# Attention matmuls of 128 and 32 columns split over row and column parts of the array

## The chip, the cores and the metric

The kernel runs on one core of a Trainium2 chip. The core's engines are named as in the profile: PE (TensorE, the matmul array; PEld is its loading of weights), DVE (VectorE), ACT (ScalarE), POOL (GpSimd) and SP (SyncE, which here only issues DMAs). The metric is the device time of one execution in microseconds (us).

## What is computed

A linear attention with a decaying state is followed by a feed-forward layer with a cosine gate. There are 4 batches, 8 heads, 768 positions and 48 values a head; the layer goes from 384 to 2048 and back.

```python
for t in range(S):
    cur = einsum('bhd,bhe->bhde', u * k_t, v_t)
    y[:, :, t] = einsum('bhd,bhde->bhe', r_t, state + cur)
    state = w[:, :, None] * state + einsum('bhd,bhe->bhde', k_t, v_t)
x = y, heads side by side, as (B*S, 384)
h = x @ w_in
out = (h * cos(h)) @ w_out
```

## The kernel before

**Chunks.** The positions are cut into chunks of 128, so there are 24 chunks (6 of each batch, chunk i belongs to batch i % 4). Inside a chunk the recurrence is turned into matmuls. k and r are transposed and multiplied by tables of powers of w (L651, L676, L702, L711; late chunks load them in strips and transpose them on DVE, L659, with POOL multiplying, L664). Then, for each of the 8 heads:

- scores: kT by rT, 128 x 128 (`mm_a`, L740). Even and odd heads use the two halves of the rows of the array and write into two PSUM banks, `Ap[0]` and `Ap[1]`. Only entries with key before query count.
- A: ACT writes the identity times r.(u k) of the head into A (`diagonal`, L730), and DVE copies the scores above the diagonal over it (`mask`, L746).
- x: the state times r (`mm_x`, L760) and v times A (`mm_x2`, L773), both with outputs of 32 columns of the array, four column groups in turn, into one bank `xp`. For L760 the state of two heads is first spread by ACT into a buffer `zt` whose other halves are zero (`spread`, L788). ACT casts x to its high part (L796), DVE subtracts for the low part (L801).
- the update of the state: k by v (`mm_z`, L812), then DVE (L820 to L823). The first chunk of a batch has no state yet, and the last needs no update.

**Feed-forward.** Blocks of three chunks (384 columns) go through 16 slices of the hidden layer. A step is nine matmuls for h (L231), a chain of ACT and DVE operations for the gate (L242, L245, L248, L251, L924, L927, L930), and nine matmuls back (L237). All numbers are split into two parts, hence three matmuls for each product.

**Weights.** They arrive as 64-bit words and are converted on ACT, DVE and POOL (L511 to L552); later each piece is loaded again to check its range (L432 to L465).

**Order.** The program does not write its order by hand. `Plan.order` simulates all engines with a cost for each operation and always takes the operation that can start first, the one with the earlier due time among equals. It also gives out the buffers of each ring (`Buf`, `Tile`). Each engine works its list strictly in that order. The first 12 chunks have negative due times and come before the first h; the other 12 are strewn among the steps of the feed-forward part. Early chunks take their PSUM banks from seven (`B_EARLY`), late ones from three (`B_ATT`). While PE has nothing to do before the first h, warm-up matmuls (L989) fill the gap.

**Loads.** SP issues one DMA for each of k, r and v of a chunk (L593, L609). Late chunks load k and r once more in strips, four DMAs each (L614), into the buffers `raw`, of which there are two and which the weights use too.

## Time and profile before

| what | value |
|---|---|
| median of 3 runs | 529.81 us (529.73 to 530.69) |
| the profiled execution's own time | 530.91 us |
| its span, first to last instruction | 529.2 us |
| mean granted PE clock | 0.997 |
| first matmul of the feed-forward part | 64.41 us |

A line of the timeline gives start, length, engine, line and operation, output and inputs, shapes and count; consecutive instructions of one kind are merged. The length of a merged line ends with a modelled end of its last matmul, which overlaps with the next line, so costs are taken from start to start. In the windows, each engine's busy time in the stretch is followed by its number of instructions. In the groups by line, the busy time and the mean time of one come first, then the engine's idle time just before them.

### The profile page before, as it was taken

What the parts mean: (1) busy time and instruction counts of PE and PEld (TensorE: products, weight loads), DVE (VectorE), ACT (ScalarE), POOL (GpSimd) and SP (SyncE); (2) the same over time, 40 slices, a digit from 0 to 9 for tenths busy, and PEclk for the clock granted to TensorE, in tenths of its full rate; (3) what the DMA queues carried; (4) which work ended last, traced back from release to release, by engine and by line L of the source; (5) the groups of instructions that cost most, each with busy time, mean ns of one, the idle gap of its engine ahead of it and who ended that gap; (6) DMA issues with size and microseconds to landing.
All of it is one profiled execution on the core that took longest, in us unless ns stands there. A gap on an engine that the chain in (4) does not pass through costs nothing.

```text
span 529.2 us, 11825 instructions
## 1 busy us (share of the span) xinstructions
PE 515.1 (97%) x4428; PEld 481.2 (91%) x4428; DVE 424.9 (80%) x835; ACT 397.8 (75%) x933; POOL 178.4 (34%) x184
## 2 busy tenths in 40 slices
PE   8999999999999999999999999999989999999995
PEld 6787799999999999999999998999989999999994
DVE  6688788889889787567898999888999889876453
ACT  3888898988789768758687785777857877766664
POOL 6766522265444344233516314033142240400000
PEclk9999999999999999999999999999999999999998
DMA  9887235668756494424675836455445555300001
GB/s 139 143 164 157 66 103 192 197 141 158 148 125 148 117 149 90 76 61 68 125 165 128 170 95 135 105 165 136 112 119 130 167 146 117 96 26 21 1 1 51
DMA packets 114979, 61.60 MB, mean 116 GB/s; under 512 B 78433, under 2 KB 110818, under 8 KB 114914
## 3 DMA queue, kind: packets, MB, share of 16 engines
q1 hardware_dynamic: 109586, 53.50, 41.6%
q0 software_dynamic: 5184, 7.08, 9.4%
q8 instruction: 36, 0.59, 0.5%
q14 instruction: 29, 0.24, 0.2%
q10 hardware_dynamic: 144, 0.20, 0.1%
HBM read 48.96 MB, written 11.80 MB: 115 GB/s over the span
## 4 chain that ended last, share of the span: by engine, by line
PE 81%; DVE 8%; ACT 5%; issue 2%; DMA 2%; POOL 1%; SPq 0%; DVEq 0%; ACTq 0%; POOLq 0%
PE bank L231 33%; PE bank L237 32%; PE bank L740 5%; PE bank L773 5%; PE bank L760 3%; PE bank L651 2%; PE bank L812 2%; DVE gl L930 2%; DMA raw<-in_moe_w_out_dram 1%; DVE f L924 1%; ACT A L730 1%; PE bank L989 1%; ACT gh L927 1%; DVE f L245 1%; ACT f L251 1%
## 5 line engine op out<-in xcount | busy, mean ns | idle before, releaser
L231 PE MATMUL bank<-xh,w_in_hi 128*128 128x384 f32 x384 | 131.8, 343 | 2.8 <-DVE f L924 2.8
L237 PE MATMUL bank<-w_out_hi,gh 128*128 128x384 f32 x384 | 131.4, 342 | 0.5 <-ACT gh L927 0.2
L237 PE MATMUL bank<-w_out_hi,gl 128*128 128x384 f32 x384 | 130.2, 339 | 0.6 <-DVE gl L930 0.6
L237 PE MATMUL bank<-w_out_lo,gh 128*128 128x384 f32 x384 | 129.5, 337 | 0.0
L231 PE MATMUL bank<-xh,w_in_lo 128*128 128x384 f32 x384 | 129.3, 337 | 0.0
L231 PE MATMUL bank<-xl,w_in_hi 128*128 128x384 f32 x384 | 128.8, 336 | 0.0
L924 DVE TENSOR_TENSOR f<-bank,f 128x384 f32<-128x384 f32 (+1 forms) x132 | 71.4, 541 | 36.5 <-ACT f L251 35.9
L930 DVE TENSOR_TENSOR gl<-f,gh 128x384 fp32r<-128x384 f32 (+1 forms) x132 | 84.2, 641 | 14.2 <-ACT gh L927 12.9
L927 ACT CAST gh<-f 128x384 fp32r<-128x384 f32 (+1 forms) x132 | 65.9, 501 | 35.9 <-DVE f L924 33.4
L248 ACT ACTIVATE f<-f 128x384 f32<-128x384 f32 (+1 forms) x132 | 67.6, 514 | 33.2 <-DVE f L245 32.6
L245 DVE SCALAR_TENSOR_TENSOR f<-bank,qi 128x384 f32<-128x384 f32 (+1 forms) x132 | 70.8, 539 | 19.4 <-ACT qi L242 19.0
L242 ACT ACTIVATE qi<-bank 128x384 int32<-128x384 f32 (+1 forms) x132 | 62.3, 475 | 26.7 <-PE bank L231 26.4
L251 ACT ACTIVATE f<-f,quarter 128x384 f32<-128x384 f32 (+1 forms) x132 | 79.6, 605 | 2.1
L231 PEld LDWEIGHTS bank<-xh,w_in_hi 128*128 128x128 f32 x384 | 72.1, 188 | 7.9 <-DVE f L924 4.5
L237 PEld LDWEIGHTS bank<-w_out_hi,gh 128*128 128x128 f32 x384 | 72.0, 187 | 4.5 <-issue 1.6
L237 PEld LDWEIGHTS bank<-w_out_hi,gl 128*128 128x128 f32 x384 | 72.0, 188 | 1.7 <-DVE gl L930 1.5
L231 PEld LDWEIGHTS bank<-xl,w_in_hi 128*128 128x128 f32 x384 | 72.2, 188 | 0.0
L231 PEld LDWEIGHTS bank<-xh,w_in_lo 128*128 128x128 f32 x384 | 72.1, 188 | 0.0
L237 PEld LDWEIGHTS bank<-w_out_lo,gh 128*128 128x128 f32 x384 | 72.0, 187 | 0.0
L730 ACT ACTIVATE A<-ident,a 128x128 f32<-128x128 f32 x192 | 59.3, 389 | 6.3 <-DVE a L721 5.8
L664 POOL TENSOR_TENSOR kT<-kT,decT_k 112x512 f32<-112x512 f32 x12 | 15.6, 1302 | 143.5 <-DVE kT L659 111.8
L542 POOL TENSOR_TENSOR f<-f,raw 128x384 int32<-128x384 int32 x32 | 39.0, 1219 | 65.1 <-DVE f L531 24.8
(88 smaller groups left out, 677.0 us busy)
## 6 DMA issues: line engine op xcount, KB each, us to landing
raw<-in_moe_w_in_dram SPq DMA_DIRECT2D x32, 384.0 KB, 3.3
raw<-in_moe_w_out_dram SPq DMA_DIRECT2D x32, 384.0 KB, 3.2
out_dram<-f POOLq DMA_DIRECT2D x36, 192.0 KB, 5.0
k<-in_k_dram SPq DMA_DIRECT2D x24, 192.0 KB, 3.7
v<-in_v_dram SPq DMA_DIRECT2D x24, 192.0 KB, 4.2
raw<-in_k_dram SPq DMA_DIRECT2D x47, 96.0 KB, 2.3
raw<-in_r_dram SPq DMA_DIRECT2D x47, 96.0 KB, 2.4
out_dram<-f SPq DMA_DIRECT2D x23, 192.0 KB, 3.9
```

Of the source, the lines that this page charges most:

```text
L231: nc.tensor.matmul(ph, a, b_, start=(i == 0), stop=(i == len(mm) - 1))
L237: nc.tensor.matmul(acc, a[:, ts], b_[:, f, :], start=(first and i == 0), stop=(last and i == 2))
L242: nc.scalar.activation(qi, ph, AF.Copy, scale=INV_2PI)
L245: nc.vector.scalar_tensor_tensor(q, ph, INV_2PI, qi, op0=ALU.mult, op1=ALU.subtract)
L248: nc.scalar.activation(q, q, AF.Abs)
L251: nc.scalar.activation(q, q, AF.Sin, scale=-TWO_PI, bias=quarter)
L542: lambda: nc.gpsimd.tensor_tensor(ai(), ai(), cn(), op=ALU.add),
L730: nc.scalar.activation(A[j]()[:, p, :], ident, AF.Copy, scale=ab()[:, h : h + 1])
L740: nc.tensor.matmul(cube(Ap[j])[:, p, :], kT()[ps, p, :], rT()[ps, p, :], start=True, stop=True)
L924: nc.vector.tensor_tensor(g()[:, cs], ph()[:, cs], q()[:, cs], op=ALU.mult)
L927: nc.scalar.copy(gh()[:, cs], g()[:, cs])
L930: nc.vector.tensor_tensor(gl()[:, cs], g()[:, cs], f32(gh())[:, cs], op=ALU.subtract)
```

## The change

The order of the heads in memory changes: the even heads take slots 0 to 3, the odd heads slots 4 to 7. For the odd heads the first and the second 64 positions of a chunk are exchanged when they are loaded, and the transposes use an identity with exchanged halves (`swap`). So while an even head's first half of keys lies in rows 0 to 63, an odd head's second half does.

- **Scores.** Each head becomes two matmuls of 64 keys: the first keys against all 128 queries, the second keys against the last 64 only. The second keys against the first queries, a quarter of the square that never counts, are not computed. Four parts of the array (two halves of rows, two halves of columns) take turns.
- **A** is stored as 64 columns on the diagonal (masked) and 64 columns across (copied by ACT, `across`). `diagonal` writes 64 columns instead of 128.
- **x.** The state is used as it lies in `zc`, so `zt` and `spread` go. State by r and v by A run in eight parts (two halves of rows, four column groups), the two halves of rows into two banks `xp[0]` and `xp[1]`. Two bf16 matmuls with zeros clear the first 64 columns and begin the sums. ACT copies one bank out, DVE adds the other.
- **Order.** In late chunks the update of the state (`mm_z`) follows x in one operation. Loads of k, r and v are three DMAs each, strips eight instead of four, w and u two each. A third raw buffer lies over the early chunks' r buffers, and the ring f has nine buffers.

```diff
-        R_r = ring("r", 2, [P, H, DP], F32)
+        r_all = att.tile([P, 2, H, DP], F32, name="r_all")
+        R_r = [Tile(r_all[:, i]) for i in range(2)]
+        raw_r = Tile(r_all.rearrange("q i h d -> q (i h d)")[:, 0 : 2 * DM].bitcast(I32).rearrange("q (f w) -> q f w", w=2))
...
-        R_f = ring("f", 8, [P, DM], F32)
+        R_f = ring("f", 9, [P, DM], F32)
...
-        R_raw = ring("raw", 2, [P, DM, 2], I32)
+        R_raw = ring("raw", 2, [P, DM, 2], I32) + [raw_r]
-        zc = [att.tile([KP, NP, D], F32, name=f"zc{b}") for b in range(B)]
-        R_zt = ring("zt", 2, [KP, NP, 2 * D], F32)
+        zc = [att.tile([KP, NP, DP], F32, name=f"zc{b}") for b in range(B)]
...
+        def load_w():
+            for a in range(2):
+                src = w.rearrange("(i j a) d -> a i j d", j=2, a=2)
+                nc.sync.dma_start(wr[2 * a : 2 * a + 2, :, 0:D], src[a])
...
+        b_0 = [Buf(B_EARLY) for _ in B_EARLY]
+        def start_banks():
+            for b_ in b_0:
+                nc.tensor.matmul(
+                    b_().rearrange("q (a t) -> q a t", a=4),
+                    warm, warm[:, None, :].to_broadcast([P, 4, P]), start=True, stop=True)
+        op(PE, -300, 1.6, start_banks, [o_dve], b_0)
...
+        def slot(h):
+            return h // 2 + 4 * (h % 2)
+        PARTS = []
+        for g in range(NK * 4):
+            n, m = divmod(g, 3)
+            for h, skip in (((2 * n, 0),), ((2 * n, 32), (2 * n + 1, -16)), ((2 * n + 1, 16),))[m]:
+                PARTS.append((h, skip, g // 4, g % 4))
+        def rounds(n, of, key=lambda x, i: 0):
+            out = {}
+            for g in range(4):
+                for i in range(2):
+                    some = [x for x in PARTS if x[3] == g and of(x, i)]
+                    assert len(some) == n
+                    for t, x in enumerate(sorted(some, key=lambda x: key(x, i))):
+                        out[t, g, i] = (i, *x)
+            return [out[t] for t in sorted(out)]
+        def second(h, i):
+            return i ^ (h % 2)
+        BY_STATE = rounds(2, lambda x, i: slot(x[0]) % 2 == i)
+        BY_V = rounds(4, lambda x, i: True, lambda x, i: second(x[0], i))
+        BY_K = [(0, 0), (2, 1), (1, 0), (3, 1), (2, 0), (0, 1), (3, 0), (1, 1)]
...
+            def load_to(dst, src):
+                t0 = c * C
+                nc.sync.dma_start(dst[:, 0:4], src[b, 0:H:2, t0 : t0 + C, :].rearrange("h t d -> t h d"))
+                for i in range(2):
+                    t1 = t0 + (1 - i) * HC
+                    nc.sync.dma_start(
+                        dst[i * HC : (i + 1) * HC, 4:H], src[b, 1:H:2, t1 : t1 + HC, :].rearrange("h t d -> t h d")
+                    )
...
-                        nc.scalar.activation(A[j]()[:, p, :], ident, AF.Copy, scale=ab()[:, h : h + 1])
+                        nc.scalar.activation(A[j]()[:, p, 0:HC], ident2, AF.Copy, scale=ab()[:, h : h + 1])
...
             def mm_a():
-                for p in range(NP):
+                for p, i in BY_K:
+                    t0 = second(p // 2, i) * HC
                     for j in range(2):
                         ps = slice(j * DP, j * DP + D)
-                        nc.tensor.matmul(cube(Ap[j])[:, p, :], kT()[ps, p, :], rT()[ps, p, :], start=True, stop=True)
+                        nc.tensor.matmul(
+                            cube(Ap[j])[i * HC : (i + 1) * HC, p, 0 : C - t0],
+                            kT()[ps, p, t0 : t0 + HC], rT()[ps, p, t0:C], start=True, stop=True, skip_group_check=True)
...
-                    A[j](), upper[:, None, :].to_broadcast([P, NP, C]), cube(Ap[j])
+                    A[j]()[:, :, 0:HC], upper[:, None, :].to_broadcast([P, NP, HC]), cube(Ap[j])[:, :, 0:HC]
...
+            def across(j):
+                return lambda: nc.scalar.copy(A[j]()[:, :, HC:C], cube(Ap[j])[:, :, HC:C])
...
             def mm_x():
+                for i in range(2):
+                    rows = slice(i * HC, (i + 1) * HC)
+                    nc.tensor.matmul(xv(i)[:, :, 0:HC], warm[rows], warm[rows, None, 0:HC].to_broadcast([HC, NK, HC]),
+                        start=True, stop=False, skip_group_check=True)
+                if c:
+                    state = zc[b].rearrange("q p e -> q (p e)")
+                    for i, h, skip, kk, g in BY_STATE:
+                        p, j = divmod(slot(h), 2)
+                        ps = slice(j * DP, j * DP + D)
+                        at = p * DP + skip
+                        nc.tensor.matmul(xv(i)[G * g : G * g + G, kk, :], state[ps, at : at + G], rT()[ps, p, :],
+                            start=False, stop=False, skip_group_check=True)
+                vf = vb().rearrange("q h d -> q (h d)")
+                for i, h, skip, kk, g in BY_V:
+                    p, j = divmod(slot(h), 2)
+                    rows = slice(i * HC, (i + 1) * HC)
+                    at = slot(h) * DP + skip
+                    t0 = second(h, i) * HC
+                    nc.tensor.matmul(xv(i)[G * g : G * g + G, kk, t0:C], vf[rows, at : at + G],
+                        A[j]()[rows, p, 0 : C - t0], start=False, stop=True, skip_group_check=True)
...
+            def mm_xz():
+                mm_x()
+                if more:
+                    mm_z()
...
+            x_y = op(ACT, due - 0.6, 0.42, lambda: nc.scalar.copy(xs(), xp[1]()[:, 0:DM]), [xo], [xp[1], xs])
+            x_s = op(DVE, due - 0.5, 0.56, lambda: nc.vector.tensor_tensor(xs(), xp[0]()[:, 0:DM], xs(), op=ALU.add),
+                [x_y], [xp[0], xs])
...
```

More of the change, by code (lines that the diff above doesn't have):

```diff
@@ L194 @@
     G = 32
+    HC = C // 2
     NQ = 24
@@ L603, in chunk @@
                 ks, rs = Buf(R_raw), Buf(R_raw)
+            rbs = [rb] if late else [rb, r_first]
             def rn():
@@ new lines, in mm_z @@
+            def mm_z():
+                z = zp()[:, 0 : NP * D].rearrange("q (p e) -> q p e", p=NP)
+                for h in range(H):
+                    p, j = divmod(h, 2)
+                    nc.tensor.matmul(z[j * DP : j * DP + D, p, :], kb()[:, h, 0:D], vb()[:, h, 0:D], start=True, stop=True)
+            more = c < CPB - 1
+            def mm_xz():
+                mm_x()
+                if more:
+                    mm_z()
+            xs = Buf(R_f)
+            x_cost = 0.1 + (0.5 if c else 0.0) + 0.75
@@ new lines, in chunk @@
+            x_after = [e_r, l_v, o_pool, o_dve, *e_A, last_z[b]]
+            if late:
+                zo = xo = op(
+                    PE,
+                    due - 0.7,
+                    x_cost + (0.5 if more else 0.0),
+                    mm_xz,
+                    [o_kd, *x_after],
+                    [rT, *xp, vb, *A] + ([kb, zp] if more else []),
+                    lat=0.3,
+                )
+            else:
+                xo = op(PE, due - 0.7, x_cost, mm_x, x_after, [rT, *xp, vb, *A], lat=0.3)
```

211 lines of the change are left out of this document (118 added, 93 removed).

## The prediction

> **What bounds the kernel now.** I read the page first, then busy time by stretch, then the order of time on PE. The page says which engine to look at, and the chain of work that ended last says the same.
>
> ```profile
> PE 515.1 (97%) x4428; PEld 481.2 (91%) x4428; DVE 424.9 (80%) x835; ACT 397.8 (75%) x933; POOL 178.4 (34%) x184
> PE 81%; DVE 8%; ACT 5%; issue 2%; DMA 2%; POOL 1%; SPq 0%; DVEq 0%; ACTq 0%; POOLq 0%
> ```
>
> PE holds 81% of the chain, so PE time taken out is worth time, if nothing else is close behind. The windows show how close it is (columns: stretch, length, then busy us of PE, PEld, DVE, ACT, POOL).
>
> ```profile
> 16.00:64.00 48.00, 46.82 (x920) 37.49 (x919) 38.33 (x74) 42.18 (x126) 30.96 (x31) 1.00 0.68 132
> 260.00:320.00 60.00, 60.00 (x521) 55.93 (x519) 54.88 (x107) 47.41 (x110) 19.78 (x18) 1.00 0.61 138
> 320.00:380.00 60.00, 59.19 (x511) 55.09 (x502) 53.11 (x100) 43.82 (x101) 17.39 (x15) 1.00 0.50 125
> 380.00:450.00 70.00, 68.33 (x605) 63.48 (x604) 63.27 (x121) 51.32 (x118) 18.06 (x17) 1.00 0.56 138
> ...
> 480.00:529.00 49.00, 42.81 (x242) 41.67 (x240) 24.04 (x57) 29.01 (x70) 0.00 (x0) 0.97 0.04 14
> ```
>
> There are two stages. Up to 64 us the first 12 chunks of the attention run alone: PE is full, ACT at 42.18 of 48 close behind. After it the feed-forward part runs with 12 late chunks strewn in: PE is full, DVE second, at 171.3 of 190 us from 260 to 450. Next, what a chunk costs PE. First the early stage, PE's timeline (start, length, line, count):
>
> ```profile
> 19.15 1.16 PE L740 MATMUL bank<-rT,kT 48*128 48x128 f32 x16
> ...
> 39.43 0.65 PE L651 MATMUL bank<-ident,k 128*112 128x128 f32 x4
> 39.92 0.60 PE L651 MATMUL bank<-ident,r 128*112 128x128 f32 x4
> 40.45 0.86 PE L760 MATMUL bank<-rT,zt 112*32 112x128 f32 x24
> 41.24 1.16 PE L740 MATMUL bank<-rT,kT 48*128 48x128 f32 x16
> 42.33 1.10 PE L773 MATMUL bank<-A,v 128*32 128x128 f32 x32
> 43.37 0.56 PE L812 MATMUL bank<-v,k 128*48 128x48 f32 x16
> 43.86 0.65 PE L651 MATMUL bank<-ident,r 128*112 128x128 f32 x4
> ...
> 61.79 1.16 PE L740 MATMUL bank<-rT,kT 48*128 48x128 f32 x16 [0.36 <-ACT kT L711]
> ```
>
> From start to start a chunk with a state takes 4.43 us of PE (39.43 to 43.86): scores L740 1.09, state by r L760 0.79, A by v L773 1.04, state update L812 0.49, the rest transposes. Chunks 3 to 12 have their scores at 19.15 to 61.79, nine steps of 4.74 us: PE is nearly the pitch there. In the main stage the same bursts stand between matmuls of 384 columns:
>
> ```profile
> 223.39 0.34 PE L237 MATMUL bank<-w_out_lo,gh 128*128 128x384 f32 x1
> 223.66 1.16 PE L740 MATMUL bank<-rT,kT 48*128 48x128 f32 x16
> 224.75 0.44 PE L237 MATMUL bank<-w_out_hi,gh 128*128 128x384 f32 x1
> 225.03 0.34 PE L237 MATMUL bank<-w_out_hi,gl 128*128 128x384 f32 x1
> ...
> 229.34 0.34 PE L237 MATMUL bank<-w_out_lo,gh 128*128 128x384 f32 x1
> 229.61 1.10 PE L773 MATMUL bank<-A,v 128*32 128x128 f32 x32
> 230.64 0.44 PE L231 MATMUL bank<-xh,w_in_hi 128*128 128x384 f32 x1
> 230.92 0.34 PE L231 MATMUL bank<-xl,w_in_hi 128*128 128x384 f32 x1
> ```
>
> A 384-column matmul normally follows the one before by 0.175 us. From 223.39 to 225.03 are 1.64; less two normal steps the scores cost 1.29, which is 0.20 more than their 1.09: that is the price of leaving the full array and coming back. For L773 the same sum is 1.58 - 0.35 = 1.23. With 0.20 added, L760 costs 0.99 and L812 0.69. How many of each fall into the main stage (groups by line, 200 to 480 us):
>
> ```profile
> L740 PE MATMUL bank<-rT,kT 48*128 48x128 f32 x192 | 13.9, 285 | 0.0
> L773 PE MATMUL bank<-A,v 128*32 128x128 f32 x384 | 13.3, 277 | 0.0
> L760 PE MATMUL bank<-rT,zt 112*32 112x128 f32 x288 | 10.4, 277 | 0.0
> L812 PE MATMUL bank<-v,k 128*48 128x48 f32 x128 | 4.5, 212 | 0.0
> ```
>
> 12 bursts each, and 8 of L812: 12 x (1.29 + 0.99 + 1.23) + 8 x 0.69 = 47.6 us.
>
> **The change: PE.** The eight matmuls of the scores leave 16 records, so an f32 matmul is two. L760's 24 records over four column groups are 6 rounds in 0.79, L773's 32 are 8 rounds in 1.04: a round of 128 columns is 0.125, with 0.04 around it. L740's 8 rounds hold only two tiles each and still take (1.09 - 0.04)/8 = 0.131: a round costs what one tile costs, however many tiles are in it. L812's rounds of 48 columns take (0.49 - 0.04)/8 = 0.056; between, 64 columns are 0.070.
> Scores: 16 matmuls in fours, two fours of 128 and two of 64 columns, two records each: 4 x 0.125 + 4 x 0.070 + 0.04 = 0.82; saves 0.27. State by r: 16 matmuls in two rounds of eight, 4 x 0.125 = 0.50. A by v: 32 in four rounds, half of them short, 0.78. The two bf16 matmuls that clear the banks, in another split of the array, aren't in the trace; between 0.04 (the margin of a burst) and 0.40 (two changes of 0.20), I take 0.20, one change. Together 0.20 + 0.50 + 0.78 + 0.04 = 1.52, and now in one burst: 1.72 in the main stage instead of 0.99 + 1.23, saves 0.50. The update follows in the same burst and saves one return, 0.20, eight times. Main stage: 12 x 0.77 + 1.6 = 10.8 us. Early: 12 x 0.27, and for the 8 chunks there with a state (the first chunk of each of the 4 batches has none) 8 x (0.79 + 1.04 - 1.52); without a state 1.02 takes the place of 1.04. That is 3.2 + 2.5 = 5.7.
> A rule against the halves: the Trainium skill, TensorEngine Tiling (Array Packing), Instruction Overhead, says that every matmul carries about 60 cycles and that a dimension already small should not be cut further. If 64 columns cost as much as 128, a chunk would lose 8 x 0.055 = 0.44, some 10 us of the 16 in all. The row of L812 speaks against it: 48 columns take less than half a round of 128.
>
> **The change: ACT and DVE.** The rows by shape:
>
> ```profile
> L730 ACT ACTIVATE A<-ident,a 128x128 f32<-128x128 f32 x192 | 59.3, 389 | 6.3 <-DVE a L721 5.8
> L788 ACT COPY zt<-zc 48x192 f32<-48x192 f32 x40 | 13.9, 348 | 2.1 <-PE bank L760 1.2
> L958 ACT COPY f<-bank 128x384 f32<-128x384 f32 x40 | 18.9, 477 | 4.7 <-PE bank L237 3.8 <-issue 0.5
> L927 ACT CAST gh<-f 128x384 fp32r<-128x384 f32 x126 | 64.3, 511 | 35.8 <-DVE f L924 33.4 <-PE bank L237 1.2 <-PE bank L231 0.7
> L927 ACT CAST gh<-f 128x128 fp32r<-128x128 f32 x6 | 1.6, 292 | 0.1
> L746 DVE COPY_PREDICATED A<-upper,bank 128x512 f32<-128x512 int32 x48 | 34.9, 741 | 8.1 <-ACT A L730 6.4 <-PE bank L812 0.7 <-PE bank L740 0.3
> L924 DVE TENSOR_TENSOR f<-bank,f 128x384 f32<-128x384 f32 x126 | 69.7, 553 | 35.4 <-ACT f L251 34.7
> L924 DVE TENSOR_TENSOR f<-bank,f 128x128 f32<-128x128 f32 x6 | 1.8, 292 | 1.2 <-ACT f L251 1.2
> ```
>
> ACT: 256 columns fewer save 0.22 (L927), so 64 fewer save 0.055, eight times 0.44; the two L788, 0.70, go where there is a state. Two copies of 256 columns come, between 0.292 and 0.477, 0.385 each, and one of 384, 0.477. Net +0.11 with a state, +0.81 without. DVE: two masks of 256 columns, midway between 0.292 and 0.553, 0.42 each instead of 0.741, -0.64; the sum of the two banks +0.55; net -0.09. So neither engine is relieved. The wait for the two new copies is PE's, and behind it stand the feed-forward matmuls; the copies are planned well ahead of it, so I put it at nothing; without that cover it costs up to one copy, 0.4, a chunk.
> The 12 late chunks in 280 us make about 8 between 260 and 450: 8 x 0.9 = 7.2 us less of PE in 190 leaves DVE, with 171.3, at 94%. The range checks among that work can slide behind 450. The way from the last attention matmul to x is one ACT and one DVE operation longer (0.477 + 0.553), at four block starts. For both I take off 1.8 of the 10.8; the bounds are 0, if checks and chain fit into DVE's gaps, and 6.5, if DVE hands back nearly all of the 7.2. 9.0 remain. The buffer that holds the sum of the banks is the ninth of a ring of eight, so it takes none away.
> Early, ACT's 42.18 of 48 grows by about 4 x 0.81 + 8 x 0.11 = 4.1 at most; its cover is the 5.8 us it is idle now. Of PE's 5.7 I take 2.3 (bounds 0 and 5.7), nearer to what ACT leaves, 1.7.
>
> **The change: SP.** A load of r, k or v goes out as three DMAs, a staged load as eight instead of four.
>
> ```profile
> 17.18 0.37 SPq L593 DMA_DIRECT2D k<-in_k_dram  x1
> 17.65 0.52 SPq L609 DMA_DIRECT2D r<-in_r_dram  x1
> ...
> 329.69 1.75 SPq L614 DMA_DIRECT2D raw<-in_k_dram  x4
> ...
> 6.30 0.62 PE L651 MATMUL bank<-ident,r 128*112 128x128 f32 x4 [0.15 <-DMA r<-in_r_dram]
> ```
>
> An issue takes 0.37 to 0.52, and four small ones 1.75: it is paid by the DMA, not by its size. Early: 9 x 0.44 = 4.0 us in a pitch of 4.74, which fits; at 0.52 it is 4.7 and just fits. Late: 25 issues, 11 us, and one chunk every 23 us (12 in 280); a third raw buffer gives them lead. At the very start w goes in two DMAs and five more issues stand ahead of the first r (6.30 in the row, so about 8.5); the decay tables hide most of it, but they start from w. With POOL's longer preparation I take 1.0 of slip (bounds 0 and 2.5).
> **Sum:** -9.0 - 2.3 + 1.0 = -10.3. The profiled execution took 530.91 (span 529.2), so 520.6; it lay 1.1 above the median of the runs, 529.81, and against that the forecast is 519.5.
>
> **The rivals.** *More arrives:* the early stage passes on all 5.7 and DVE costs nothing in the main one: -10.8 - 5.7 + 1.0 = -15.5, 514.3; bursts with less margin reach 512. For it: PE 46.82 of 48. Against: ACT 42.18.
> *The gain stops at DVE and ACT:* main stage 10.8 - 6.5 = 4.3, early stage nothing, slip 1.0: -3.3, 526.5. For it: 54.88 of 60. Against: DVE has 25 idle us after 480, where checks can go.
> *SP becomes the bound of the early stage (slower):* if nine issues of smaller DMAs take 0.65 each they set a pitch of 5.8 instead of 4.74, +11.7 over 11 chunks, and the first loads slip 2.5: -9.0 + 11.7 + 2.5 = +5.2, 535. It decides from about 0.6 an issue. For it: SP works its queue in order and waits there for buffers. Against: 0.37 in most rows.
> *Row and column parts don't run beside each other (slower):* every round of eight or four falls into two. Scores 1.60 (+0.51), the x burst 3.0 against 2.22 (+0.78), main 12 x 1.29 - 1.6 = 13.9, early some 16: +30, 560. It decides from where a new round takes 1.3 old ones. L740 shows two row parts together, L773 four column parts; no row shows both at once. The Trainium skill, TensorE: Matmul & The Clock Gate, Measured speedup vs the span model, gives 10.6 times for 16 parts in both directions, which speaks against this rival.
>
> **How the numbers follow.** Forecast (516 to 523) 0.48; more arrives 0.18; gain stops 0.19; within 0.2% 0.04; SP 0.07; parts not together 0.04. 0.2% is 1.1 us, about what a measurement of this kernel can tell from none. Faster 0.85, same 0.04, slower 0.11. For 8 in 10 the range leaves out the two slower rivals and the edge of the others: 512 to 527.
>
> **What would show it.** Scores' bursts near 0.9 instead of 1.16, one burst of about 1.6 us in place of L760 and L773, with eight starts a round; PE busy 14 to 17 us less. First feed-forward matmul at 62 to 64 instead of 64.41. DVE above 93% from 260 on with few PE gaps. Wrong if rounds of 64 columns take 0.1 or more, if SP issues stand above 0.6, or if PE waits grow by over 6 us.

## The result: slower by 7.4%

| | before | after |
|---|---|---|
| median | 529.81 us | 568.95 us (567.11 to 572.17, 4 runs) |
| ratio, 95% interval | | 1.0741 (1.069 to 1.0792) |
| profiled execution, its span | 530.91, 529.2 | 572.17, 570.4 |
| mean granted PE clock | 0.997 | 0.965 |
| first feed-forward matmul | 64.4 | 94.1 |
| main stage (from it to the start of PE's last instruction) | 458.1 | 468.8 |

So 29.7 us of the 41.2 by which the span grew lie ahead of the first feed-forward matmul, 10.7 in the main stage and 0.8 behind it. First the profile page of the changed kernel, busy time and chain:

```profile
PE 527.1 (92%) x5817; PEld 490.1 (86%) x5817; DVE 444.5 (78%) x861; ACT 398.9 (70%) x967; POOL 183.2 (32%) x188
PE 46%; DVE 17%; SPq 11%; DMA 10%; ACT 8%; issue 4%; POOL 3%; POOLq 0%; DVEq 0%; ACTq 0%
```

PE's share of the chain fell from 81% to 46%. SP's queue and the DMAs, together 2% before, hold 21%. DVE went from 8% to 17%. These are the two places to look at. The windows of the changed kernel say when (stretch, length, busy us of PE, PEld, DVE, ACT, POOL, then PE's clock, DMA share, GB/s):

```profile
16.00:64.00 48.00, 37.21 (x982) 27.82 (x978) 24.91 (x54) 29.43 (x95) 21.05 (x21) 0.87 0.55 98
64.00:94.00 30.00, 25.18 (x653) 20.20 (x654) 16.69 (x35) 16.45 (x54) 14.30 (x14) 0.77 0.49 104
...
290.00:410.00 120.00, 116.11 (x1383) 109.35 (x1363) 113.49 (x213) 87.28 (x207) 39.95 (x35) 1.00 0.59 138
```

In the early stage every engine is idle for long: PE 37.21 of 48, warm-up matmuls included, where it was 46.82, and ACT 29.43 where it was 42.18. And PE's clock is down to 0.87 and 0.77. In the main stage DVE is at 113.49 of 120, and PE has gaps that it didn't have. What the early stage waits for stands in SP's timeline and in the list of waits (engine, line, what it waited for: us, times, longest) of the changed kernel:

```profile
30.73 0.55 SPq L682 DMA_DIRECT2D r_all<-in_r_dram  x1
31.37 1.25 SPq L685 DMA_DIRECT2D r_all<-in_r_dram  x2
32.72 0.56 SPq L682 DMA_DIRECT2D v<-in_v_dram  x1
33.32 1.25 SPq L685 DMA_DIRECT2D v<-in_v_dram  x2
34.69 0.54 SPq L682 DMA_DIRECT2D k<-in_k_dram  x1
35.32 1.25 SPq L685 DMA_DIRECT2D k<-in_k_dram  x2
36.67 1.44 SPq L682 DMA_DIRECT2D r_all<-in_r_dram  x1
```

```profile
POOL f L784 <- DMA r_all<-in_r_dram: 30.7, 9, 5.6
...
PE bank L749 <- DMA r_all<-in_r_dram: 10.5, 12, 2.1
```

SP issues one DMA after the other with hardly a gap. From 30.73 to 36.67 are the three loads of one chunk: 5.94 us for nine issues. PE's timeline at the same time:

```profile
33.04 0.90 PE L839 MATMUL bank<-rT,kT 48*64 48x128 f32 x32
...
37.17 0.71 PE L1133 MATMUL bank<-warm 128*128 128x256 bf16 x5
...
38.98 0.90 PE L839 MATMUL bank<-rT,kT 48*64 48x128 f32 x32
```

From scores to scores 33.04 to 38.98: 5.94 us again. The early stage runs at SP's pace, and PE fills the rest with warm-up matmuls. Over the whole stage the pitch is longer still: the scores of the first and the twelfth chunk start at 11.29 and 90.69, eleven steps of 7.22. SP is at it all the time: the 108 issues of the 12 chunks stand from 2.42 to 84.48, 0.76 each. Ten of them took 0.98 to 1.95, together some 8.5 us more than ten of the others, and PE's clock was at half in several stretches.

PE's own work did become shorter. The bursts of the changed kernel in its main stage:

```profile
262.83 0.34 PE L239 MATMUL bank<-w_out_lo,gh 128*128 128x384 f32 x1
263.10 0.90 PE L839 MATMUL bank<-rT,kT 48*64 48x128 f32 x32
...
264.21 0.34 PE L239 MATMUL bank<-w_out_hi,gl 128*128 128x384 f32 x1
...
269.61 0.34 PE L239 MATMUL bank<-w_out_lo,gh 128*128 128x384 f32 x1
269.88 0.26 PE L870 MATMUL bank<-warm 64*128 64x192 bf16 x2
270.07 0.67 PE L884 MATMUL bank<-rT,zc 48*32 48x128 f32 x32
270.53 1.03 PE L894 MATMUL bank<-A,v 64*32 64x128 f32 x64
271.49 0.56 PE L907 MATMUL bank<-v,k 128*48 128x48 f32 x16
...
272.26 0.33 PE L239 MATMUL bank<-w_out_hi,gl 128*128 128x384 f32 x1
```

Read as in the prediction, the scores cost 264.21 - 262.83 - 0.35 = 1.03 (1.29 before), and the burst of x with the update 272.26 - 269.61 - 0.35 = 2.30 (before 0.99 + 1.23 + 0.69 = 2.91). That is 0.26 for the scores of 12 chunks, 0.61 for the 8 with an update and 0.41 for the 4 without, 9.6 us if every burst were like these. Added up over all bursts of the main stage (below) 6.8 us are saved. More than that is lost elsewhere.

**Three sums used below.** *Gaps*: wherever two feed-forward matmuls follow each other by over 0.15 us more than the normal step of 0.175, the excess, added up over the trace. *Bursts*: for each burst of attention matmuls between feed-forward matmuls the cost as just read, added up; a wait of PE right behind a burst falls in here and not into the gaps. *DVE above normal*: for each DVE instruction after the first feed-forward matmul that took over 0.15 longer than the lower quartile of its line and shape, the excess, added up.

| profiled run | first matmul | main stage | gaps (number) | bursts | DVE above normal |
|---|---|---|---|---|---|
| before | 64.4 | 458.1 | 5.4 (9) | 49.3 | 19.2 |
| after | 94.1 | 468.8 | 17.6 (19) | 42.5 | 36.8 |
| e1, one DMA a load, four strips | 67.9 | 461.6 | 10.8 (14) | 41.7 | 36.9 |
| e12, one DMA a load, eight strips | 68.1 | 464.9 | 16.6 (20) | 41.8 | 36.9 |
| e8, e1 with POOL's addition on DVE | 67.4 | 457.6 | 8.8 (15) | 43.2 | 23.1 |
| e9, e1 with three edits | 68.5 | 463.1 | 8.0 (13) | 48.1 | 23.4 |
| e11, before with joined bursts | 64.3 | 455.3 | 6.9 (13) | 44.5 | 21.6 |

Each row is one execution; those of the changed kernel and of e1 took 3.2 and 2.3 us more than the medians of their runs, so a difference of 2 or 3 us between two rows shows nothing by itself.

### The profile page after: what moved, and what is told of

Its sections match the earlier page's. It is cut to its first block, busy times and chain, and to the rows that moved or that the text cites. A ratio compares the mean times of both kernels' runs of the same rounds, so it can differ in the third digit from the quotient of the medians.

```text
span 570.4 us, 15083 instructions
## 1 busy us (share of the span) xinstructions
PE 527.1 (92%) x5817; PEld 490.1 (86%) x5817; DVE 444.5 (78%) x861; ACT 398.9 (70%) x967; POOL 183.2 (32%) x188
## 4 chain that ended last, share of the span: by engine, by line
PE 46%; DVE 17%; SPq 11%; DMA 10%; ACT 8%; issue 4%; POOL 3%; POOLq 0%; DVEq 0%; ACTq 0%
PE bank L233 20%; PE bank L239 20%; DMA r_all<-in_r_dram 5%; SPq L712 4%; DVE gl L1074 4%; SPq L685 4%; DVE f L1068 2%; SPq L682 2%; DVE f L247 2%; ACT gh L1071 2%; PE bank L894 2%; ACT f L253 1%; ACT f L250 1%; PE bank L839 1%; DVE w_out_lo L605 1%
## 5 line engine op out<-in xcount | busy, mean ns | idle before, releaser
L239 PE MATMUL bank<-w_out_hi,gl 128*128 128x384 f32 x384 | 132.1, 344 | 6.3 <-DVE gl L1074 6.1
L1074 DVE TENSOR_TENSOR gl<-f,gh 128x384 fp32r<-128x384 f32 (+1 forms) x132 | 85.6, 650 | 12.2 <-ACT gh L1071 10.8
L1071 ACT CAST gh<-f 128x384 fp32r<-128x384 f32 (+1 forms) x132 | 65.9, 501 | 41.2 <-DVE f L1068 37.8
L250 ACT ACTIVATE f<-f 128x384 f32<-128x384 f32 (+1 forms) x132 | 67.9, 516 | 34.8 <-DVE f L247 34.1
L247 DVE SCALAR_TENSOR_TENSOR f<-bank,qi 128x384 f32<-128x384 f32 (+1 forms) x132 | 70.7, 538 | 16.9 <-ACT qi L244 16.6
L828 ACT ACTIVATE A<-ident,a 128x64 f32<-128x64 f32 x192 | 50.0, 338 | 5.0 <-DVE a L819 4.9
L1117 POOL DMA_DIRECT2D out_dram<-f x36 | 32.0, 1101 | 42.1 <-ACT f L1102 37.1
```

The costliest lines, as they stand in the source:

```text
L239: nc.tensor.matmul(acc, a[:, ts], b_[:, f, :], start=(first and i == 0), stop=(last and i == 2))
L247: nc.vector.scalar_tensor_tensor(q, ph, INV_2PI, qi, op0=ALU.mult, op1=ALU.subtract)
L250: nc.scalar.activation(q, q, AF.Abs)
L828: nc.scalar.activation(A[j]()[:, p, 0:HC], ident2, AF.Copy, scale=ab()[:, h : h + 1])
L1071: nc.scalar.copy(gh()[:, cs], g()[:, cs])
L1074: nc.vector.tensor_tensor(gl()[:, cs], g()[:, cs], f32(gh())[:, cs], op=ALU.subtract)
```

## The experiments

The theory after the result: in the early stage SP's issues are the pace, and in the main stage PE waits for DVE, which is held up by DMAs and by POOL. The rivals: the exchange itself is dear (transposes with `swap`, copies), the plan's wrong numbers spoil the order, or the small DMAs are slow on the way rather than at SP. All ratios are against runs of the kernel before on the same chip.

### e1_one_dma: one DMA a load, four strips

```diff
-                nc.sync.dma_start(dst[:, 0:4], src[b, 0:H:2, t0 : t0 + C, :].rearrange("h t d -> t h d"))
-                for i in range(2):
...
+                nc.sync.dma_start(dst, src[b, :, c * C : (c + 1) * C, :].rearrange("h t d -> t h d"))
```

> The changed kernel, but r, k and v are loaded by one DMA each and the strips by four, as before; heads and halves then lie in the natural order, so the values are those of other heads and positions. Theory SP (the number of DMAs that SP issues, about 0.65 us each in a row, holds the early stage, and its lateness puts the planned order out of step later): first feed-forward matmul at 60 to 65 us instead of 94, time 515 to 525. Rival PE (the smaller matmuls themselves or the longer way to x cost the time): still above 550, first feed-forward matmul above 85.

Measured: 537.95 us (535.82 to 540.25), ratio 1.0155 (1.0121 to 1.0189). The first feed-forward matmul came at 67.9, so 26.2 of the 29.7 us belong to the split of the loads. But neither the time nor the first matmul reached the ranges expected (515 to 525, 60 to 65): the main stage, 461.6, is still longer than before, though its bursts are as short as in the changed kernel. Its longest gap, in the timeline of e1:

```profile
126.23 3.22 DVE L605 TENSOR_TENSOR w_out_lo<-f,w_out_hi 128x384 fp32r<-128x384 f32 x1
126.40 2.62 POOL L595 TENSOR_TENSOR f<-f,raw 128x384 int32<-128x384 int32 x2
129.38 0.54 DVE L1061 TENSOR_TENSOR f<-bank,f 128x384 f32<-128x384 f32 x1
...
129.97 0.69 PE L233 MATMUL bank<-xh,w_in_hi 128*128 128x384 f32 x1 [2.81 <-DVE f L1061]
```

A DVE subtraction that normally takes 0.55 took 3.22: as long as POOL's two additions beside it. Behind it in DVE's queue stood the gate's multiplication L1061, behind that PE, 2.81 us. None of these lines belongs to the change. In the kernel before no gap between feed-forward matmuls is longer than 1.83 us; that it is the new order alone that makes them meet is argued, not shown (e7). The Trainium skill, SBUF — State Buffer, section SBUF: two separate sides, describes such a wait: DVE and GpSimd share a pair of SBUF ports under an exclusive lock for a whole instruction, and a DVE operation with two SBUF operands takes part in it when the GpSimd operation reads SBUF. The row agrees so far: both operands of L605 are in SBUF, while L1061, which reads a bank, keeps its 0.54. That L605 is held through two of POOL's operations, though it started before the first, is not said there; the row shows it.

Behind the gap PE is slow for a while (windows of e1):

```profile
129.00:136.00 7.00, 6.03 (x19) 6.03 (x20) 6.17 (x13) 4.85 (x11) 0.02 (x1) 0.52 0.53 141
136.00:143.00 7.00, 7.00 (x42) 7.00 (x40) 5.03 (x11) 5.65 (x14) 4.00 (x5) 0.99 0.59 101
```

From 129 to 136 PE's clock is 0.52. Of these 7 us the first 0.97 are the end of the gap; in the rest there are 19 matmuls at 0.32 each, which would take 3.3 us at the normal step. That the gap brought this about is not shown: another gap of the same length had no such stretch behind it (last section).

### e2_before_split: the kernel before with three DMAs a load

```diff
+                nc.sync.dma_start(dst[:, 0:4], src[b, 0:4, t0 : t0 + C, :].rearrange("h t d -> t h d"))
+                for i in range(2):
+                    t1 = t0 + i * 64
+                    nc.sync.dma_start(dst[i * 64 : (i + 1) * 64, 4:H], src[b, 4:H, t1 : t1 + 64, :].rearrange("h t d -> t h d"))
```

> The kernel before with nothing changed but that each load of r, k and v is three DMAs of the same bytes. Theory SP: the pitch of an early chunk goes from 4.7 to 6.5 us, first feed-forward matmul at 85 to 95, time 550 to 565. Rival PE: SP has room, as the prediction said; within 5 us of 529.8.

Measured: 555.69 us (552.91 to 558.04), ratio 1.0509 (1.0455 to 1.0563), first feed-forward matmul at 89.2, main stage 457.6. Nothing but the split of the loads differs from the kernel before, and 25 us of the early stage's loss are there. Its SP queue:

```profile
30.68 0.55 SPq L594 DMA_DIRECT2D v<-in_v_dram  x1
31.33 1.25 SPq L597 DMA_DIRECT2D v<-in_v_dram  x2
32.69 0.55 SPq L594 DMA_DIRECT2D k<-in_k_dram  x1
```

One load from start to start (30.68 to 32.69) is 2.0 us, as in the changed kernel. So the exchange has no part in it. Nor are the small DMAs slow on the way (issues by tile, KB each, median us from issue to landing; the kernel before, then e2):

```profile
k<-in_k_dram SPq DMA_DIRECT2D x24, 192.0 KB, 3.7
```

```profile
k<-in_k_dram SPq DMA_DIRECT2D x48, 48.0 KB, 2.5
```

Once issued they land sooner than the large ones; it is the issuing that takes the time.

### e3_no_exchange: the changed kernel with the heads in natural order

```diff
-            return h // 2 + 4 * (h % 2)
+            return h
...
-            return i ^ (h % 2)
+            return i
...
-                    nc.tensor.transpose(d[0:KP, p, :], flat(src, p), ident if p < 2 else swap)
+                    nc.tensor.transpose(d[0:KP, p, :], flat(src, p), ident)
```

Loads, strips, w and u go as before; `zc` gets 16 columns in front.

> The changed kernel without the exchanged halves: heads in natural order, the halves of rows carry unequal numbers of columns, all loads as before (one DMA, strips four, one for w and u). Theory SP: about as fast as with one DMA and exchange, 517 to 527, scores about 1.0 us instead of 0.85, v by A hardly slower because the issue of 64 records, 0.015 us each, holds it already. Rival PE: above 550.

Measured: 541.18 us (540.23 to 541.68), ratio 1.0224 (1.0194 to 1.0253); first matmul at 71.2, main stage 462.4, gaps 10.6. A miss. Without the exchange two long rounds no longer meet, so the scores take 1.02 from start to start; but the 14 us by which it misses the range can't come from that. Exchange and loads are both taken back here and the main stage stays long, so they aren't all of its loss. The early stage too is late with the loads of before: PE's clock was at half for 6.8 us from 11.3 on, behind a pause. The clearing of the banks ahead of it was the suspect, and e6 tests it.

### e4_plan_told: the changed kernel, the plan told what SP's issues cost

```diff
-                l_ks = op(SP, due - 6.2, 2.2, load_s(ks, k), ahead, [ks], lat=4.0, line=ln)
+                l_ks = op(SP, due - 6.2, 3.9, load_s(ks, k), ahead, [ks], lat=4.0, line=ln)
...
-            l_k = op(SP, due - 5.2, 1.35, load(kb, k), ahead, [kb], lat=2.6, line=ln)
+            l_k = op(SP, due - 5.2, 2.1, load(kb, k), ahead, [kb], lat=2.6, line=ln)
```

> The changed kernel with nothing changed but the costs that the planner takes for SP: 2.1 instead of 1.35 us for a load, 3.9 instead of 2.2 for strips. Theory SP with the plan out of step: the early stage stays at 90 to 95 us, the main stage, 469 us now, loses 5 to 15, time 553 to 565. Rival (the main stage is lost to the loads themselves or to the longer way to x): no change, 565 to 573.

Measured: 568.3 us (566.83 to 569.89), ratio 1.0742 (1.0703 to 1.0781). Against the 568.95 of the changed kernel that is nothing, as the rival had it (565 to 573). A miss for the theory that knowing the price helps: work that SP can't do in time isn't made less by another order. (The other three costs, of r's strips and of loading r and v, changed in the same way.)

### e5_sum_in_bank: x from the bank

```diff
-                lambda: nc.vector.tensor_tensor(xs(), xp[0]()[:, 0:DM], xs(), op=ALU.add),
+                lambda: nc.vector.tensor_tensor(xp[0]()[:, 0:DM], xp[0]()[:, 0:DM], xs(), op=ALU.add),
```

> The kernel of e1_one_dma (each load one DMA, so its numbers aren't the reference's), with one thing changed: DVE writes the sum of the two banks back into the bank instead of into SBUF, and the high and the low part of x are taken from the bank, so the subtraction for the low part no longer reads two operands from SBUF. Theory A, the longer way to x costs the main stage through the port that DVE and POOL share: DVE's time above normal after the first feed-forward matmul falls from 36.9 us to 30 or less, the main stage from 461.6 to 457 to 460, total 533 to 536. Theory B, the collisions come from the order in which the plan puts everybody's work, the new operations add little to them: 33 to 40 us above normal, main stage 459 to 465, total 536 to 541.

Measured: 535.06 us (533.81 to 540.78), ratio 1.0098 (1.0071 to 1.0125). The subtraction for the low part, in the changed kernel and in e5 (groups by line: busy, mean ns):

```profile
L950 DVE TENSOR_TENSOR xl<-f,xh 128x384 fp32r<-128x384 f32 x24 | 17.1, 714 | 2.0 <-ACT xh L945 2.0
```

```profile
L943 DVE TENSOR_TENSOR xl<-bank,xh 128x384 fp32r<-128x384 f32 x24 | 13.2, 550 | 0.4 <-ACT xh L938 0.3
```

With one operand from the bank it takes 550 ns, as before the change (24 in 13.2 us), with two from SBUF 714 on average. DVE above normal fell to 25.8 and the main stage to 458.6, both as theory A said, and so is the total. The profiled run took 540.78, 5.7 above the median, with two stretches of half clock in the early stage, so its first matmul, 70.9, isn't typical of the median.

### e6_start_later: banks cleared behind the transposition of w

```diff
-        op(PE, -300, 1.6, start_banks, [o_dve], b_0)
...
+        for b_ in b_0:
+            op(PE, -94, 0.23, start_bank(b_), [o_dve, o_wT], [b_])
```

> The kernel of e1_one_dma with the seven matmuls that clear the banks at the start moved behind the transposition of w (one operation a bank instead of one for all). Theory A, they hold up the decay tables by about 1.2 us, and the pause before the first scores costs as much again: first feed-forward matmul at 65 to 66.5 instead of 67.9, total 1.5 to 3 us less than 537.95 if the main stage stays. Theory B, the first stage is late for another reason (more instructions on PE, the longer way to x): first feed-forward matmul still 67 to 68.5.

Measured: 536.08 us (535.44 to 537.75), ratio 1.0127 (1.0099 to 1.0155), first matmul at 66.8: between the two theories. Of the 3.5 us by which e1 starts its main stage late, 1.1 go with the clearing, by one profile each. Where the other 2.4 lie is open. The main stage changed as well, 458.3, though nothing of it was touched but the order that the plan makes of it.

### e7_before_told: the kernel before, one planned cost changed

```diff
-            last_A[0] = o_A = op(PE, due - 1.7, 1.1, mm_a, [e_k, e_r], [kT, rT, *Ap], lat=0.3)
+            last_A[0] = o_A = op(PE, due - 1.7, 0.8, mm_a, [e_k, e_r], [kT, rT, *Ap], lat=0.3)
```

> The kernel before with the same work, one number of the plan changed: the scores of a chunk are planned at 0.8 us instead of 1.1, as the changed kernel plans them. Theory order: the kernel before owes part of its time to an order that happens to keep DVE and POOL apart; with another order DVE's time above normal in the main stage rises from 19.2 us to 25 to 38, PE's stalls from 5.4 to 8 to 12, total 532 to 538. Theory work: the order matters little and the time stays at 529 to 531.

Measured: 532.09 us (530.33 to 533.2), ratio 1.0049 (1.0028 to 1.0069). The time is in the range of the theory of order, but not for its reason: DVE above normal stayed at 17.8 and the gaps at 5.3. The new order put the first feed-forward matmul at 52.5, with chunks left over for the main stage, which grew to 471.0. So the order alone moves this kernel by half a per cent, and a difference of 2 or 3 us between two runs of this study may be no more than that. That the changed order alone brings the collisions of DVE and POOL isn't shown by it.

### e8_add_on_dve: POOL's addition moved to DVE

```diff
-                POOL,
...
-                lambda: nc.gpsimd.tensor_tensor(ai(), ai(), cn(), op=ALU.add),
+                DVE,
...
+                lambda: nc.vector.tensor_tensor(ai(), ai(), cn(), op=ALU.add),
```

> The kernel of e1_one_dma with the 32 additions of the weights' conversion moved from POOL to DVE (DVE's sum of integers can lose their lowest bits, so the numbers aren't the reference's). Up to about 260 us POOL then has little besides the attention, and the long waits of DVE behind it at 113.4, 126.2 and 164.5 can't come. Theory A, the stalls of PE up to 260 us are DVE waiting for POOL: DVE's time above normal between 64 and 260 falls from 15.3 to 6 or less, stalls from 10.8 to 4 to 7, the stretch of half clock at 129.3 goes, main stage 453 to 457, total 530 to 534. Theory B, DVE itself is what PE waits for: 17.6 us more work on DVE make the stalls longer, main stage 462 to 470, total 538 to 546.

Measured: 534.12 us (533.0 to 538.86), ratio 1.0104 (1.0066 to 1.0143). DVE above normal between 64 and 260 us fell from 15.3 to 0.9, the gap at 126 and the half clock behind it are gone, and the main stage fell by 4.0 to 457.6, though DVE got 32 additions more. So the waits behind POOL were a real cost, and DVE's own work wasn't the bound there. Total and main stage end just above theory A's ranges. The gaps are 8.8 and not the 4 to 7 expected: those behind 260 us, where POOL works for the attention, stayed (22.2 us of DVE above normal).

### e9_together: the three edits at once

```diff
+                lambda: nc.vector.tensor_tensor(xp[0]()[:, 0:DM], xp[0]()[:, 0:DM], xs(), op=ALU.add),
...
+            op(PE, -94, 0.23, start_bank(b_), [o_dve, o_wT], [b_])
...
+                lambda: nc.vector.tensor_tensor(ai(), ai(), cn(), op=ALU.add),
```

> The three edits of e5_sum_in_bank, e6_start_later and e8_add_on_dve together, on the kernel of e1_one_dma (the numbers aren't the reference's, for the reasons given there). Theory A, the longer way to x, the clearing at the start and DVE's waits behind POOL are three separate losses: they add up, 537.95 less 2.9, 1.9 and 3.8 gives 529.4, so 528 to 532, with a main stage of 453 to 456. Theory B, each edit only gave the plan another order, and the gains don't add: 533 to 537.

Measured: 540.95 us (538.05 to 542.47), ratio 1.0213 (1.018 to 1.0245). Above the ranges of both theories: the gains don't add, and the three edits together are no faster than none. The first feed-forward matmul came at 68.5, the main stage took 463.1. DVE above normal did fall, to 23.4, and the gaps to 8.0. One of them alone is 2.9 us long (timeline of e9):

```profile
448.97 1.61 POOL L755 TENSOR_TENSOR rT<-rT,decT_r 112x512 f32<-112x512 f32 x1
449.35 2.63 DVE L509 TENSOR_TENSOR f<-f,f 128x384 f32<-128x384 f32 x1
450.53 1.03 POOL L785 TENSOR_TENSOR k<-k,dec_k 128x384 f32<-128x384 f32 x1
...
454.22 0.44 PE L233 MATMUL bank<-xh,w_in_hi 128*128 128x384 f32 x1 [2.74 <-DVE f L1060]
```

It is the same pattern with other lines: L509, an operation of the range check, sits through two of POOL's, and the gate waits behind it. Two longer waits stand right behind bursts, so they are in the 48.1 of the bursts (e1: 41.7):

```profile
75.27 0.45 PE L233 MATMUL bank<-xh,w_in_hi 128*128 128x384 f32 x1 [3.37 <-ACT w_in_hi L600]
...
297.78 0.44 PE L233 MATMUL bank<-xh,w_in_hi 128*128 128x384 f32 x1 [3.17 <-DVE f L1060]
```

The second is the gate again. The first is another kind, a piece of the weights that ACT hasn't converted yet. So the plan's new order brought waits of its own, not all of them of DVE behind POOL.

### e10_before_two: the kernel before with two DMAs a load

```diff
+                nc.sync.dma_start(dst[:, 0:4], src[b, 0:4, t0 : t0 + C, :].rearrange("h t d -> t h d"))
+                nc.sync.dma_start(dst[:, 4:H], src[b, 4:H, t0 : t0 + C, :].rearrange("h t d -> t h d"))
```

> The kernel before with each load of r, k and v in two DMAs (four heads each). Theory A, an issue of SP in an unbroken row costs 0.6 to 0.65 us whatever its size: six of them take 3.6 to 3.9 us of a pitch of 4.74, they fit, first feed-forward matmul at 64 to 67, total 529 to 532.5. Theory B, splitting itself is what hurts (later arrival, smaller transfers): half of the 26 us of e2_before_split, first feed-forward matmul at 72 to 78, total 537 to 543.

Measured: 527.75 us (526.74 to 528.58), ratio 0.9968 (0.9951 to 0.9984), first matmul at 64.5. That is below theory A's range and far from theory B's. Six issues a chunk fit, nine of e2's kind don't: the loss sets in between, as a bound does, and splitting by heads costs nothing. The Trainium skill, DMA: Bandwidth & Descriptors, section Rules for kernel authors, advises one transfer over 128 partitions in place of two to halves of them. The loads of the change do the opposite for the odd heads, and e2, which does so too, lost 25 us; e10, split by heads over all partitions, lost nothing. But e2 has nine issues and e10 six, so no run tells the halves from the number. Its SP queue has gaps:

```profile
34.93 0.37 SPq L594 DMA_DIRECT2D v<-in_v_dram  x1
35.39 0.46 SPq L595 DMA_DIRECT2D v<-in_v_dram  x1
36.52 0.75 SPq L594 DMA_DIRECT2D k<-in_k_dram  x1
```

The second of two loads here mostly takes 0.46 to 0.50 right behind the first, the halves of e2 and of the change 0.59 to 0.62. An estimate from these rows: nine issues of e10's kind, 0.55 from start to start, would be 4.95 us, a little more than the pitch of 4.74, and not 5.94.

### e11_before_joined: the joined bursts alone

```diff
+            def mm_xz():
+                mm_x()
+                mm_x2()
+                if more:
+                    mm_z()
...
+                zo = xo2 = op(PE, due - 0.7, 1.83 + (0.5 if more else 0.0), mm_xz, ...)
```

(State by r only where there is one; for late chunks alone.)

> The kernel before with one part of the change alone: in the late chunks the state by r, v by A and the update of the state are one operation of PE, so they stand in one burst; loads, scores and x are as before. Theory A, a border between the attention and the feed-forward matmuls costs 0.19 us: 44 bursts become about 25, which saves 3.6 us of the main stage, 458.1 to 453.5 to 455.5, total 525 to 527.5. Theory B, the new order costs as much in waits of PE as the borders save: main stage 457 to 462, total 528.5 to 533.

Measured: 526.99 us (526.03 to 529.72), ratio 0.9965 (0.9947 to 0.9983). The time is that of theory A, and the main stage, 455.3, is at the upper end of its range. The timeline:

```profile
228.04 0.34 PE L237 MATMUL bank<-w_out_lo,gh 128*128 128x384 f32 x1
228.31 0.86 PE L760 MATMUL bank<-rT,zt 112*32 112x128 f32 x24
228.99 1.08 PE L773 MATMUL bank<-A,v 128*32 128x128 f32 x32
230.00 0.56 PE L799 MATMUL bank<-v,k 128*48 128x48 f32 x16
...
230.78 0.34 PE L237 MATMUL bank<-w_out_hi,gl 128*128 128x384 f32 x1
```

230.78 - 228.04 - 0.35 = 2.39. The eight parts, two banks, two more copies and the sum of the change reach 2.30 for the same work. So of the 0.61 by which this burst became shorter, 0.52 came from joining and 0.09 from the parts.

### e12_strips_eight: which DMAs the main stage minds

```diff
-                nc.sync.dma_start(dst[:, 0:4], src[b, 0:H:2, t0 : t0 + C, :].rearrange("h t d -> t h d"))
...
+                nc.sync.dma_start(dst, src[b, :, c * C : (c + 1) * C, :].rearrange("h t d -> t h d"))
```

The loads' edit of e1_one_dma alone; the eight strips stay.

> The changed kernel with each load of r, k and v as one DMA in natural order, and its eight strips kept (heads of loads and strips don't match, so the numbers aren't the reference's); e1_one_dma has four strips as well. It tells where the 7.2 us lie by which the changed kernel's main stage (468.8) is longer than that of e1_one_dma (461.6). Theory strips, DVE's transposition waits for eight DMAs that SP issues too slowly, and the gate's operations stand behind it: the main stage stays at 465 to 469, a transposition waits over 1 us for its strips, total 541 to 546. Theory loads, it is the 25 issues of a late chunk together, and 19 are few enough: no such wait, main stage 460 to 463, first feed-forward matmul at 67 to 69 in both cases, total 536 to 540.

Measured: 542.41 us (541.7 to 543.02), ratio 1.023 (1.0201 to 1.0259). Strips: 4.5 us more than e1 by the medians (4.0 by the ratios), and two transpositions wait for them, 2.79 and 1.4 us. Ahead of the first the last strip landed 4.5 us after its issue at 179.82, and the transposition started at 184.64. The same in the changed kernel itself:

```profile
203.26 3.70 SPq L712 DMA_DIRECT2D raw<-in_r_dram  x8
...
211.30 1.08 DVE L757 STREAM_TRANSPOSE rT<-raw 128x512 f32<-128x512 f32 x1 [2.50 <-issue]
...
212.23 0.53 DVE L1074 TENSOR_TENSOR gl<-f,gh 128x384 fp32r<-128x384 f32 x1
```

```profile
212.82 0.66 PE L239 MATMUL bank<-w_out_hi,gl 128*128 128x384 f32 x1 [2.24 <-DVE gl L1074]
```

The eight strips of r leave SP until 206.96, the transposition that needs them starts at 211.30, and DVE does nothing for 2.50 us ahead of it. The gate's subtraction stands behind it in DVE's queue, and PE waits 2.24 us. The main stage of e12, 464.9, ends just under the range of that theory (465 to 469). The other 3.9 us up to the changed kernel's 468.8 are 1.0 of gaps, 0.7 of bursts and for the rest half clock: 10.2 us of the changed kernel's main stage had it and 3.4 of e12's. Why isn't known.

### e13_joined_two: e10 and e11 together

```diff
+                nc.sync.dma_start(dst[:, 4:H], src[b, 4:H, t0 : t0 + C, :].rearrange("h t d -> t h d"))
...
+                zo = xo2 = op(PE, due - 0.7, 1.83 + (0.5 if more else 0.0), mm_xz, ...)
```

> The kernel before with the two edits that made it faster together: one burst for x and the update in late chunks (e11_before_joined, 526.99 against 529.41) and two DMAs a load (e10_before_two, 527.75). If the two gains are separate they add: 2.4 and 1.7 give 525.3, so 524 to 526.5, first feed-forward matmul at 64 to 65, main stage 453.5 to 455.5. If the gain of the two DMAs was only another alignment of DVE and POOL, it doesn't add: 526.5 to 529.

Measured: 526.8 us (525.15 to 531.12) beside 530.01 of the kernel before on that chip, ratio 0.9947 (0.9924 to 0.9969); main stage 454.1. If the gains added, the ratio would be 0.9965 x 0.9968 = 0.9933, and that lies in the interval; but so does that of one edit alone, 0.9965. The time lies in the range for gains that don't add (526.5 to 529), the main stage in the other. Whether they add stays open. e10, e11 and e13 are the versions that beat both kernels, by 0.3 to 0.5%.

## Why the prediction was wrong

- **The step that failed is SP's term**, "Early: 9 x 0.44 = 4.0 us in a pitch of 4.74, which fits". The rows of 0.37 and 0.52 were issues with pauses around them, and the four strips, 0.44 each, were DMAs of another form: in a row of eight they take 0.46 each in the changed kernel too (203.26, 3.70). The loads of the change take 0.54 to 0.62 in their unbroken row, and 0.05 to 0.1 passes to the next issue, which the sum left out: nine took 5.94. The rival *SP becomes the bound of the early stage* named the mechanism and, with 0.65 an issue, the price; the measured pitch of 5.94 is its 5.8. It was given 7%, with the argument "0.37 in most rows" against it (18 of the 36 loads), and those rows don't show the state that the change makes. Nor was 0.6 an issue needed: 4.74 over nine is 0.53 from start to start. Its +14.2 was also too small: the stage got 29.7 longer. Eleven steps longer by 1.2 are 13.2 of that, the ten longer issues some 8.5; the rest, half clock among it, wasn't told apart.
- **The early saving of PE, 2.3, did not arrive either.** With one DMA a load (e1) the first feed-forward matmul came 3.5 later and not 1.3 earlier. From 16 to 64 us PE spends 6.5 on warm-up matmuls there, before 3.8, so at least part of the time that PE saved went into filling. What holds the stage instead is open.
- **Scores, state, x: right.** 1.03 where 0.82 + 0.20 was forecast, 2.30 for x with the update where 1.72 + 0.49 = 2.21 was. Inside, A by v is 0.96 (270.53 to 271.49) and not 0.78: its 64 records take 0.015 each, so the halved columns gain little. That is 0.12 for each round of eight records, and "rounds of 64 columns take 0.1 or more" was one of the signs of being wrong; the short rounds of the scores do take 0.07, (0.83 - 0.04 - 0.5)/4. State by r, 0.46, and the clearing, 0.19, were as forecast or better. The rival *row and column parts don't run beside each other* is refuted.
- **The main stage's other half: wrong in size.** For DVE and the longer way to x 1.8 was taken off, bounds 0 and 6.5. The gaps alone grew by 12.2 (5.4 to 17.6), and 26 feed-forward matmuls at half clock, 0.32 a step instead of 0.175, cost 3.8. The bursts saved 6.8 (49.3 to 42.5) and not the 10.8 of the sum: the order before had already joined three of them, which had saved it 0.8, and some of the changed kernel's took longer than those shown, the first one 3.33 with a wait for weights (before: 1.89). That makes 9.2 of the 10.7; the last 1.5 are smaller excesses of single steps. e12 and e1 give strips 4.0 to 4.5 us of the total. e5 and e8 gave 2.9 and 3.8 for x's two SBUF operands and for POOL's additions, but each came with another order, and together with e6 they gave nothing (e9), so these two aren't shown to be separate prices. The prediction looked for DVE's load and found 94% bearable. What the traces show instead of load is which instruction stands in DVE's queue ahead of the gate, held up by a DMA or by POOL.
- **ACT**: in the changed kernel not the bound of the early stage; it idles more than before.
- **The start**: the slip of 1.0 was put down to the two DMAs of w and to POOL. The first scores did start 1.3 later (9.99 to 11.29), but e6 gives 1.1 to the clearing of the banks, which the prediction doesn't name there. That the size fits is luck. 2.4 us of e1's early stage have no cause shown.
- **The signs**: issues above 0.6 and waits of PE above 6 us were named as what would prove it wrong, and both came. DVE is at 95% from 290 to 410, as forecast, but with many gaps instead of few. "PE busy 14 to 17 us less" was no good sign: PE's busy time rose by 12.0, since warm-up matmuls and matmuls at half clock count as busy.

## What to carry to other kernels

Price a DMA issue from start to start, by rows of DMAs of the same form in which the queue has no pause, and compare issues x that price with the pitch of the stage, before a load is cut into pieces; here six by heads fit, and nine with halves of the partitions cost 25 us. Before an array is split more finely, price the borders between two kinds of matmul: of the 0.61 by which the burst of x and the update became shorter, joining gave 0.52. On an engine that works in order, ask of each new or moved instruction what it can be held up by and what stands behind it, since one operation of 0.5 us that took 3.2 stopped PE for 2.8.

## What was not expected of the hardware

- An issue of SP isn't paid by the bytes: in the unbroken row of the changed kernel the loads of 96 KB (L682) mostly take 0.54 to 0.60 and the halves of 48 KB (L685) 0.59 to 0.62, while its strips, 48 KB too, take 0.46 in a row of eight. No half took less than 0.59 in the whole execution. Which part of that is the form of the DMA and which the full queue isn't shown.
- A DVE operation on two SBUF operands can take as long as POOL's operations beside it: 3.22 instead of 0.55 beside two additions, 2.63 beside L755 and L785.
- After a gap of 2.97 us (e1) PE ran at half clock for 6.8 us, 19 matmuls at 0.32 instead of 0.175, so 2.8 us more were lost. Another gap of 2.98 us (at 153.0 of the changed kernel) had no such stretch behind it, and one of 2.40 (at 212.8) had one of 3.4 us.
